# Masks by TensorE, late scaling and signs by ScalarE in the first steps of a fused attention and two-layer kernel

## The chip, the cores and the metric

The kernel runs on one core of one Trainium2 chip. The metric is the device time of one execution in microseconds; below it is the median of three runs. The profile is of one execution of its own.

## The reference

Three layers follow each other. Attention with 4 batches, 8 heads, 576 tokens and 64 dimensions keeps for each query the 32 largest scores; a dense layer of 512 to 2048 to 512 with a gated activation follows, and then a layer of eight experts, of which each token takes one.

```python
scores = scale * np.matmul(q, k.transpose(0, 1, 3, 2))
kth = np.partition(scores, -top_k, axis=-1)[..., -top_k:-top_k + 1]
scores = np.where(scores >= kth, scores, -1000000000.0)
scores = scores - np.max(scores, axis=-1, keepdims=True)
attn = np.exp(scores)
attn = attn / (np.sum(attn, axis=-1, keepdims=True) + 1e-09)
x = np.matmul(attn, v)                      # then tokens x 512
h = x @ w_in
g = h * np.clip(h + 3.0, 0.0, 6.0) / 6.0
x = g @ w_out
# experts: argmax of normalised logits; out = gate * (relu(x @ w1[e]) @ w2[e])
```

The dense layer's weights are float64 and are turned into float32 on the chip, as a rounded high part and a low part.

## The kernel before

The attention is cut into 72 units of 128 queries and two heads. A loop of 76 steps runs as a pipeline over them: step i scores unit i, selects the 32 largest of unit i−1, prepares the mask of unit i−2, takes the exponentials of units i−2 and i−3, turns the result of unit i−4 by transposes. In odd steps the products with v of units i−5 and i−4 are made. Eight units fill 256 tokens of x, which then go through the dense layer in eight pieces, one a step; so TensorE gets its main work from step 12 on. The expert layer follows after the loop.

The order of instructions is written out by hand: each step runs through a list of names, `FIRST` in steps 0 to 11, `MID` to step 20, then `ODD` and `THEN`. Each engine takes its instructions strictly in that order, and SyncE issues the DMAs in that order.

The names that matter here, with their lines: `score0`, `score1` (L435, TensorE) make the scores of half the keys for both heads in the one PSUM tile `ps_sc`; `take0`, `take1` (L446, ScalarE) copy them to the unit's tile `s`; `pairs` (L455 to L459, five VectorE operations) compares the halves and so needs `take1` and the second half in PSUM; `pick0` to `pick3` (L474, L477, VectorE) select; `bounds` (L482, L484, GpSimd) turns the 32nd largest into a bias. `bend` (L488, ScalarE) writes z, which is 0 for a kept score and huge for another one; `mask` (L492, GpSimd) subtracts z from s; `expo` (L498, ScalarE) takes the exponential in place and sums each row; `guard` (L502) and `inverse` (L505) invert the sums; `scale` (L512, ScalarE for the first 16 units) multiplies the row. `turn` (L525, TensorE) and `keep` (L530, ScalarE) transpose by way of two PSUM banks; `values` (L543, TensorE) multiplies by v; `xh` (L560, ScalarE) and `xl` (L575, VectorE) split the product.

In the same steps the float64 weights come in pieces of 128x512, one a step in steps 0 to 2 and then two, as pairs of 32-bit words. `load` fetches a piece; `one` (L241, VectorE) shifts the high word by three bits and clears the top two bits; `two` (L248, VectorE) merges sign and top exponent bit; `round` (L256, ScalarE) scales the low word to a rounding count; `add` (L261, GpSimd) adds it. One step later `hi` (L269, ScalarE) rounds to the high part, `low` (L273, GpSimd) subtracts, and `store` (L277) writes the low part to DRAM. The four buffers `wf` that `one` writes come free when the store of two steps' earlier piece has landed.

Of the kernel before, what the change touches and what calls it, by code (L numbers as in the profile page):

```python
# [38 lines left out]
EARLY = 16  # L39
PLAIN = 1  # L40
# [3 lines left out]
FIRST = ("hi0 s10 expo0 lows hi1 turn0 one0 s11 s20 low0 round0 two0 ship keep0 turn1 expo1 guard bend0 keep1 add0 turn2 load0 "  # L44
         "store0 one1 load_k inverse keep2 prep mask0 pick0 round1 score0 gate take0 scale two1 bend1 load_q swish large values xh "
         "score1 pick1 pick2 aside s21 add1 load1 xl pick3 need_v low1 take1 store1 pairs mask1 bounds small")
MID = ("lows turn0 hi0 turn1 low0 s10 s11 ship keep0 one0 keep1 expo0 two0 pick0 load_k turn2 store0 one1 pick1 expo1 hi1 guard "
       "round0 bend0 two1 score0 pick2 keep2 low1 s20 take0 gate bend1 inverse add0 score1 values take1 round1 scale swish mask0 "
       "large s21 add1 xh pick3 need_v prep xl mask1 load_q bounds small store1 load0 load1 pairs aside")
# [49 lines left out]
def layers(tc: tile.TileContext, qt, kt, v, w_in, w_out, embt, tau, w1, w2, out, y_dram, yq_dram, g_dram, tbl, xq_dram, lo_dram, flag, pools, consts):  # L99
# [33 lines left out]
    ps_y = st.enter_context(tc.tile_pool(name="ps_y", bufs=2, space=PSUM))  # L133
    ps_t = st.enter_context(tc.tile_pool(name="ps_t", bufs=1, space=PSUM))
    bank_h = ps_h.tile([128, 512], F32, name="bank_h")
    bank_a = Held(ps_a, consts).tile([128, 2, CH], F32, name="bank_a")
# [85 lines left out]
    def w_load(n):  # L222
        src, dst = wpairs[n]
        single = src.dtype == F32
        if single:
            raw = stg.tile([128, 2, 256], F32, tag="st", name="w32")
            nc.sync.dma_start(out=raw, in_=src)
        else:
            raw = stg.tile([128, 512, 2], I32, tag="st", name="w64")
            nc.sync.dma_start(out=raw.rearrange("p (a n) two -> p a n two", a=2), in_=src.bitcast(I32).rearrange("p a (n two) -> p a n two", two=2))  # L230
        ent_[n] = dict(dst=dst, raw=raw, single=single, rounded=True)

    def w_one(n):
        e = ent_[n]
        raw = e["raw"]
        e["both"] = mp.tile([128, DM], F32, tag="wf", name="wf", bufs=4)
        if e["single"]:
            nc.vector.tensor_copy(e["both"], raw.rearrange("p a n -> p (a n)"))
            return
        e["words"] = t = e["both"].bitcast(I32)  # L240
        nc.vector.tensor_scalar(t, raw[:, :, 1], 3, 0x3FFFFFFF, op0=ALU.logical_shift_left, op1=ALU.bitwise_and)  # L241

    def w_two(n):
        e = ent_[n]
        if e["single"]:
            return
        raw, t = e["raw"], e["words"]
        nc.vector.scalar_tensor_tensor(t, raw[:, :, 1], -0x40000000, t, op0=ALU.bitwise_and, op1=ALU.bitwise_or)  # L248
        if not e["rounded"]:
            nc.vector.scalar_tensor_tensor(t, raw[:, :, 0], 29, t, op0=ALU.logical_shift_right, op1=ALU.bitwise_or)  # L250

    def w_round(n):
        e = ent_[n]
        if e["rounded"] and not e["single"]:
            raw = e["raw"]
# [276 lines left out]
    avs = {}  # L532

    def values(i):
# [3 lines left out]
        avs[i] = av = half_a()[:, :128]  # L538
# [23 lines left out]
    def finish_low(i):  # L562
# [10 lines left out]
        c = slice(128 * (t % 2), 128 * (t % 2) + 128)  # L573
        xh, xl = [x[:, p, c] for x in xt[b, t // 2]]
        nc.vector.tensor_tensor(xl, av, xh.bitcast(F32), op=ALU.subtract)  # L575
        if p == 3 and t % 2:
# [11 lines left out]
    def push_group(X, gs):  # L588
# [292 lines left out]
    def step(i, last):  # L881
# [15 lines left out]
        def after(o):  # L897
            if last:
# [6 lines left out]
                   pairs=lambda: at_(0, pairs), values=lambda: both(values), xh=lambda: both(finish), xl=lambda: both(finish_low))  # L905
# [30 lines left out]
    if True:  # L936
        last = None
        with tc.manual_schedule():
# [6 lines left out]
            make_identity(nc, ident)  # L945
            nc.vector.memset(half, 0.5)
# [453 lines left out]
```

## Time and profile before

| | |
|---|---|
| median of three runs | 1007.87 us (1005.36 to 1010.01) |
| profiled execution | 1007.83 us |
| its span | 1005.8 us |
| TensorE busy in the span | 934.8 us, 93% |
| VectorE | 778.1 us, 77% |
| ScalarE | 712.8 us, 71% |
| GpSimd | 637.9 us, 63% |

The shares are means over stages with different limits. In the first tenth of the span VectorE, ScalarE and GpSimd are busy almost throughout and TensorE about half the time; from 175 us on TensorE is. The span is from the first to the last instruction; the execution's own time is 2.03 us longer.

### The profile page before, as it was taken

To read this page: it belongs to the slowest core of one execution; us is meant where nothing else is said; L and a number is where in the kernel's file an instruction comes from. 1 tells how busy PE (TensorE), PEld (TensorE's weight loads), DVE (VectorE), ACT (ScalarE), POOL (GpSimd) and SP (SyncE) were. 2 spreads that over 40 slices of the span, in tenths; PEclk is the share of its full clock that TensorE was granted. 3 is DMA by queue.
4 is the path that set the end of the run, shared out by engine and by line. 5 is a ranking of instruction groups with operands and counts; after the bars stand their busy time and mean duration, and the time that the engine had idled before them with its cause. 6 is when DMAs were issued, how large, how long until landed. Compare 5 with 4: busy or idle time off the path is not lost. (4 is left out here: it accounts for less than half of the span.)

```text
span 1005.8 us, 20687 instructions
## 1 busy us (share of the span) xinstructions
PE 934.8 (93%) x7128; PEld 820.3 (82%) x7128; DVE 778.1 (77%) x2364; ACT 712.8 (71%) x1441; POOL 637.9 (63%) x786
## 2 busy tenths in 40 slices
PE   3656688999999999999999999999999999999997
PEld 1433467989899899998998988889898988999986
DVE  7999999899989989989989899882134354666660
ACT  5899889888889788789778787785335454555551
POOL 5889899677778788688788666665333453134210
PEclk9966799999999999999999999999999999999998
DMA  7655676664456754456665476477586467767730
GB/s 251 211 177 162 213 237 234 207 202 149 141 168 195 249 184 131 137 189 192 221 177 146 143 227 202 139 237 203 172 262 223 133 226 263 242 200 239 255 124 23
DMA packets 100689, 193.21 MB, mean 192 GB/s; under 512 B 16189, under 2 KB 42448, under 8 KB 100575
## 3 DMA queue, kind: packets, MB, share of 16 engines
q1 hardware_dynamic: 95983, 181.74, 56.3%
q0 software_dynamic: 4448, 10.00, 3.2%
q8 instruction: 58, 0.95, 0.4%
q14 instruction: 56, 0.46, 0.1%
q10 hardware_dynamic: 144, 0.07, 0.0%
HBM read 163.64 MB, written 24.92 MB: 187 GB/s over the span
## 5 line engine op out<-in xcount | busy, mean ns | idle before, releaser
L492 POOL TENSOR_TENSOR s<-s,z 128x576 f32<-128x576 f32 x144 | 191.4, 1330 | 61.6 <-ACT z L488 61.0
L607 PE MATMUL bank_h<-xh,vh 128*128 128x256 f32 x576 | 171.6, 298 | 0.0
L607 PE MATMUL bank_h<-xh,lo 128*128 128x256 f32 x576 | 163.7, 284 | 0.0
L607 PE MATMUL bank_h<-xl,vh 128*128 128x256 f32 x576 | 163.6, 284 | 0.0
L474 DVE MAX8 A<-left 128x8 f32<-128x288 f32 (+1 forms) x288 | 159.5, 594 | 0.0
L525 PE MATMUL bank_t<-both,s 128*128 128x128 f32 x648 | 108.1, 290 | 30.8 <-ACT pt L530 18.1
L525 PEld LDWEIGHTS bank_t<-both,s 128*128 128x128 f32 x648 | 81.2, 148 | 53.2 <-ACT pt L530 24.2
L530 ACT COPY pt<-bank_t 128x384 f32<-128x384 f32 x216 | 101.5, 478 | 26.2 <-PE bank_t L525 26.2
L626 POOL TENSOR_TENSOR gl<-u,gh 128x512 fp32r<-128x512 f32 x72 | 93.1, 1293 | 41.6 <-ACT gh L623 41.5
L642 PE MATMUL y<-wh,gh 128*128 128x512 f32 x288 | 116.5, 405 | 0.0
L488 ACT ACTIVATE z<-s,nb 128x576 bf16<-128x576 f32 x144 | 112.2, 780 | 4.4 <-POOL nb L482 4.3
L446 ACT COPY s<-ps_sc 128x576 f32<-128x576 f32 x143 | 92.3, 645 | 32.5 <-PE ps_sc L439 11.0
L498 ACT ACTIVATE s<-s,nb 128x576 f32<-128x576 f32 x144 | 113.0, 786 | 1.5 <-POOL s L492 1.5
L642 PE MATMUL y<-lo,gh 128*128 128x512 f32 x288 | 113.5, 394 | 0.0
L642 PE MATMUL y<-wh,gl 128*128 128x512 f32 x288 | 113.2, 393 | 0.0
L607 PEld LDWEIGHTS bank_h<-xl,vh 128*128 128x128 f32 x576 | 111.2, 193 | 0.3
L607 PEld LDWEIGHTS bank_h<-xh,vh 128*128 128x128 f32 x576 | 111.1, 193 | 0.3
L607 PEld LDWEIGHTS bank_h<-xh,lo 128*128 128x128 f32 x576 | 110.7, 192 | 0.0
L1038 POOL DMA_INDIRECT out_dram<-ob,idt x21 | 25.8, 1228 | 123.4 <-ACT ob L1031 92.3
L514 POOL TENSOR_SCALAR s<-s,sums 128x576 f32<-128x576 f32 x112 | 82.5, 748 | 20.7 <-DVE sums L505 20.2
L543 PE MATMUL bank_a<-pt,vt 128*64 128x128 f32 (+1 forms) x1600 | 93.7, 275 | 0.9 <-ACT pt L530 0.9
L615 ACT ACTIVATE u<-bank_h,half 128x512 f32<-128x512 f32 x72 | 50.0, 694 | 61.8 <-PE bank_h L607 61.8
(266 smaller groups left out, 2611.6 us busy)
## 6 DMA issues: line engine op xcount, KB each, us to landing
lo<-lo_dram SPq DMA_DIRECT2D x144, 512.0 KB, 4.6
a<-in_moe_w_dram SPq DMA_DIRECT2D x64, 512.0 KB, 6.1
vt<-in_v_dram SPq DMA_DIRECT2D x28, 320.0 KB, 4.4
w<-in_moe_w_in_dram SPq DMA_DIRECT2D x16, 512.0 KB, 3.9
w<-in_moe_w_out_dram SPq DMA_DIRECT2D x16, 512.0 KB, 4.3
lo_dram<-wf SPq DMA_DIRECT2D x32, 256.0 KB, 2.7
qraw<-in_q_dram SPq DMA_DIRECT2D x48, 128.0 KB, 2.9
krs<-in_k_dram SPq DMA_DIRECT2D x16, 288.0 KB, 4.7
```

Of the source, the lines that this page charges most:

```text
L446: nc.scalar.copy(sbuf[i % NS][:, :, HS * g:HS * g + HS], ps_[i][:, :, :HS])
L474: nc.vector.max(A[:, n, 8 * r:8 * r + 8], src[:, n, :w])
L488: nc.scalar.activation(zb_[n], tile_of(i, n), AF.Relu, bias=sel[i][1][:, n, 1:2], scale=-BIG)
L492: nc.gpsimd.tensor_tensor(s, s, zb_[n], op=ALU.subtract)
L498: nc.scalar.activation(s, s, AF.Exp, bias=sel[i][1][:, n, 0:1], scale=SCALE, accum_out=sums[i][:, n:n + 1])
L514: nc.gpsimd.tensor_scalar(x, x, rv[:, n:n + 1], 1.0, op0=ALU.mult, op1=ALU.mult)
L525: nc.tensor.transpose(pp[:, 128 * k:128 * k + 128], e[:, 128 * (3 * c + k):128 * (3 * c + k) + 128], ident)
L530: nc.scalar.copy(pts[i][:, 3 * c:3 * c + 3, :].rearrange("p k n -> p (k n)"), tb_.pop((i, c))[:, :384])
L543: nc.tensor.matmul(av[64 * n:64 * n + 64, c0:c1], vt[:, k, 64 * n:64 * n + 64], pt[:, k + 5 * n if k < 4 else 4, c0:c1], start=(o == 0), s ...
L607: nc.tensor.matmul(ph[:, a, :], w, x[:, k, :], start=(k == 0 and n == 0), stop=(k == 3 and n == 2))
L626: nc.gpsimd.tensor_tensor(state[q][1], state.pop((q, "u")).rearrange("p (a n) -> p a n", a=2), state[q][0].bitcast(F32), op=ALU.subtract)
L642: nc.tensor.matmul(state["y"][o], x[:, a, c], w, start=(f == 0 and n == 0), stop=(f == 15 and n == 2))
```

## The change

It has four parts, all in steps 0 to 11.

For the first nine units (`VEILED`) the mask is put on by TensorE, under the new name `veil`: s times the identity plus z times the negative identity (in `tri`, whose later contents come at step 24) into the PSUM tile `bank_y`, 288 columns at a time; the exponential reads that tile. `bank_y` is one tile of two banks and takes the place of the two buffers of the dense layer's output. Both heads' masks use it in turn.

For the first eight units (`NORMED`) the exponentials are not scaled. `values` also multiplies the inverted sums, broadcast, by the identity, so that the other half of its PSUM bank holds the factor for each query; `xh` copies product and factor together, `xl` multiplies them on GpSimd, and the new `xe` splits the result, on ScalarE and GpSimd.

For eight weight pieces (`SIGNED`, the second piece in steps 3 to 10) `two` runs on ScalarE: a sign pass gives plus or minus 1.0, `round` adds 2^23, and the bits of both, added to the shifted word by two GpSimd operations, make up sign and top bits.

`FIRST` has another order: `low0` stands behind `add0`, `inverse` behind `pick0`, `veil1` behind `turn0`, and `veil0` between `score0` and the copy.

```diff
+NORMED = 8
+SIGNED = tuple(range(4, 20, 2))
+VEILED = 9
...
-FIRST = ("hi0 s10 expo0 lows hi1 turn0 one0 s11 s20 low0 round0 two0 ship keep0 turn1 expo1 guard bend0 keep1 add0 turn2 load0 "
+FIRST = ("hi0 s10 expo0 lows hi1 turn0 veil1 one0 s11 s20 round0 two0 ship keep0 turn1 expo1 guard bend0 keep1 add0 low0 turn2 load0 "
...
-    ps_y = st.enter_context(tc.tile_pool(name="ps_y", bufs=2, space=PSUM))
+    ps_y = st.enter_context(tc.tile_pool(name="ps_y", bufs=1, space=PSUM))
+    bank_y = ps_y.tile([128, 2, DM], F32, name="bank_y")
...
+        if e["signed"]:
+            nc.vector.tensor_scalar(t, raw[:, :, 1], 3, None, op0=ALU.logical_shift_left)
+            return
...
+        if e["signed"]:
+            nc.scalar.activation(raw[:, :, 1].bitcast(F32), raw[:, :, 1], AF.Sign)
+            return
         nc.vector.scalar_tensor_tensor(t, raw[:, :, 1], -0x40000000, t, op0=ALU.bitwise_and, op1=ALU.bitwise_or)
...
-            nc.scalar.activation(raw[:, :, 0], raw[:, :, 0].bitcast(U32), AF.Copy, scale=2.0 ** -29)
+            nc.scalar.activation(raw[:, :, 0], raw[:, :, 0].bitcast(U32), AF.Copy, bias=2.0 ** 23 if e["signed"] else 0.0, scale=2.0 ** -29)
...
-            nc.gpsimd.tensor_tensor(e["words"], e["words"], e["raw"][:, :, 0], op=ALU.add)
+            for k in (1, 0) if e["signed"] else (0,):
+                nc.gpsimd.tensor_tensor(e["words"], e["words"], e["raw"][:, :, k], op=ALU.add)
...
+    def veil(i, n):
+        if i >= VEILED:
+            return
+        s = tile_of(i, n)
+        for g in range(2):
+            c = slice(HS * g, HS * g + HS)
+            nc.tensor.matmul(bank_y[:, g, :HS], ident, s[:, c], start=True, stop=False)
+            nc.tensor.matmul(bank_y[:, g, :HS], tri, zb_[n][:, c], start=False, stop=True)
...
     def expo(i, n):
...
-        s = tile_of(i, n)
-        nc.scalar.activation(s, s, AF.Exp, bias=sel[i][1][:, n, 0:1], scale=SCALE, accum_out=sums[i][:, n:n + 1])
+        s = x = tile_of(i, n)
+        if i < VEILED:
+            s, x = s.rearrange("p (g c) -> p g c", g=2), bank_y[:, :, :HS]
+        nc.scalar.activation(s, x, AF.Exp, bias=sel[i][1][:, n, 0:1], scale=SCALE, accum_out=sums[i][:, n:n + 1])
...
     def scale(i):
+        if i < NORMED:
+            return
...
+        if i < NORMED:
+            sh = both_[:, 128:]
+            halves[i] = both_
+            rv = sums.pop(i)
+            for n in range(2):
+                nc.tensor.matmul(sh[64 * n:64 * n + 64, :], rv[:, n:n + 1].broadcast_to([128, 64]), ident, start=True, stop=True)
...
     def finish(i):
...
+        if i < NORMED:
+            nc.scalar.copy(norm_[:, i % 2, :], halves.pop(i))
+            return
...
     def finish_low(i):
...
+        if i < NORMED:
+            x = norm_[:, i % 2, :]
+            nc.gpsimd.tensor_tensor(x[:, :128], x[:, :128], x[:, 128:], op=ALU.mult)
+            return
...
+    def finish_early(i):
+        if i >= NORMED:
+            return
+        x = norm_[:, i % 2, :128]
...
+        nc.scalar.copy(xh, x)
+        nc.gpsimd.tensor_tensor(xl, x, xh.bitcast(F32), op=ALU.subtract)
...
-                state["y"] = [ps_y.tile([128, DM], F32, tag="y", name="y") for _ in gs]
+                state["y"] = [bank_y[:, o, :] for o in range(len(gs))]
...
+            nc.gpsimd.tensor_scalar(tri, ident, -1.0, None, op0=ALU.mult)
```

Where this puts the work, engine by engine. TensorE in an odd step, before: third transpose (L525), first score (L435), two units' values (L543), second score.

```order
L525 MATMUL bank_t_122<-both,s_146 128x128 x3
L435 MATMUL ps_sc<-kpl,qpl 128x288 x2
L543 MATMUL bank_a<-pt,vt 64x128 x20
L435 MATMUL ps_sc<-kpl,qpl 128x288 x2
L525 MATMUL bank_t_123<-both,s_147 128x128 x3
```

And after, at the same place (L551 transposes, L446 scores, L507 and L508 the mask, L572 the factors, L577 values):

```order
L551 MATMUL bank_t_123<-both,s_149 128x128 x3
L446 MATMUL ps_sc<-kpl,qpl 128x288 x2
L507 MATMUL bank_y<-s_147,both 128x288
L508 LDWEIGHTS tri
L508 MATMUL bank_y<-z_152,tri 128x288
...
L572 MATMUL bank_a<-both,sums 64x128 x2
L577 MATMUL bank_a<-pt,vt 64x128 x10
L572 MATMUL bank_a<-both,sums 64x128 x2
L577 MATMUL bank_a<-pt,vt 64x128 x10
L446 MATMUL ps_sc<-kpl,qpl 128x288 x2
L551 MATMUL bank_t_124<-both,s_146 128x128 x3
```

Between the two scores there stand now a mask of the next unit (shown for one of its two halves) and the factors; the other head's mask stands behind the first transpose.

ScalarE from the second rounding to the end of an odd step, before: rounding (L256), first copy (L446), both scalings (L512), z (L488), two casts (L560), second copy.

```order
L256 ACTIVATE w_437<-w_437 128x512
L446 COPY s_146<-ps_sc 128x2x288
L512 ACTIVATE s_147<-s_147,sums 128x576 x2
L488 ACTIVATE z_152<-s_148,nb 128x576
L560 CAST xh<-bank_a 128x128 x2
L446 COPY s_146<-ps_sc 128x2x288
```

And after (L266 rounding, L457 copies, L256 the sign, L499 z, L584 product and factor, L629 the split):

```order
L266 ACTIVATE w_453<-w_453 128x512
L457 COPY s_147<-ps_sc 128x2x288
L256 ACTIVATE w_453<-w_453 128x512
L499 ACTIVATE z_153<-s_149,nb 128x576
L584 COPY norm<-bank_a 128x256 x2
L457 COPY s_147<-ps_sc 128x2x288
L629 CAST xh<-norm 128x128 x2
```

The scalings are gone, the sign pass is in their place, and the split has moved behind the second copy.

GpSimd in a step, before: a sum's guard (L502), add (L261), mask (L492), add, low part (L273), mask, bounds (L482, L484), low part.

```order
L502 TENSOR_SCALAR sums<-sums 128x2
L261 TENSOR_TENSOR wf<-wf,w_400 128x512
L492 TENSOR_TENSOR s_148<-s_148,z_151 128x576
L261 TENSOR_TENSOR wf<-wf,w_437 128x512
L273 TENSOR_TENSOR wf<-wf,wh 128x512
L492 TENSOR_TENSOR s_148<-s_148,z_152 128x576
L482 TENSOR_TENSOR nb<-A,kb 128x4
L484 TENSOR_TENSOR viol<-A 128x4
L273 TENSOR_TENSOR wf<-wf,wh 128x512
```

And after, in an even step (L526 guard, L272 adds, L284 low parts, L493 and L495 bounds):

```order
L526 TENSOR_SCALAR sums<-sums 128x2
L272 TENSOR_TENSOR wf<-wf,w_502 128x512
L284 TENSOR_TENSOR wf<-wf,wh 128x512
L272 TENSOR_TENSOR wf<-wf,w_567 128x512 x2
L284 TENSOR_TENSOR wf<-wf,vh 128x512
L493 TENSOR_TENSOR nb<-A,kb 128x4
L495 TENSOR_TENSOR viol<-A 128x4
```

The masks are gone, the second piece has two adds, and the first low part now stands behind the first add; in odd steps two products (L613) stand ahead of the second low part and two subtractions (L630) behind it.

## Rows read from the trace of the kernel before

**Rows 1.** busy us by engine (PE, PEld, DVE, ACT, POOL), then PEclk, DMA, GB/s

```profile
50.00:62.50 12.50, 5.40 (x25) 3.03 (x23) 12.40 (x38) 12.50 (x27) 11.91 (x14) 0.70 0.52 164
...
175.00:200.00 25.00, 24.96 (x199) 22.72 (x198) 22.46 (x82) 21.21 (x49) 17.48 (x25) 1.00 0.62 214
```

**Rows 2.** VectorE in order of time: start, us, line, operation, out<-in, shapes

```profile
22.97 0.45 DVE L455 TENSOR_TENSOR ps_sc<-ps_sc,s 128x288 f32<-128x288 f32 x1
...
49.52 0.48 DVE L575 TENSOR_TENSOR xl<-bank_a,xh 128x128 fp32r<-128x128 f32 x2
...
51.25 0.45 DVE L455 TENSOR_TENSOR ps_sc<-ps_sc,s 128x288 f32<-128x288 f32 x1
...
53.50 0.42 DVE L241 TENSOR_SCALAR wf<-w 128x512 int32<-128x512 int32 x1
...
55.95 0.73 DVE L248 SCALAR_TENSOR_TENSOR wf<-w,wf 128x512 int32<-128x512 int32 x1
...
56.61 0.51 DVE L474 MAX8 A<-top 128x8 f32<-128x144 f32 x2
...
60.49 0.44 DVE L455 TENSOR_TENSOR ps_sc<-ps_sc,s 128x288 f32<-128x288 f32 x1
...
109.19 0.45 DVE L455 TENSOR_TENSOR ps_sc<-ps_sc,s 128x288 f32<-128x288 f32 x1
...
111.95 1.64 DVE L248 SCALAR_TENSOR_TENSOR wf<-w,wf 128x512 int32<-128x512 int32 x1
```

**Rows 3.** ScalarE in order of time, steps 5 and 6

```profile
49.05 0.43 ACT L560 CAST xh<-bank_a 128x128 fp32r<-128x128 f32 x2 [1.14 <-PE bank_a L543]
...
49.73 0.64 ACT L446 COPY s<-ps_sc 128x576 f32<-128x576 f32 x1 [0.25 <-PE ps_sc L435]
...
50.27 0.62 ACT L269 CAST wh<-wf 128x512 fp32r<-128x512 f32 x1
...
55.16 0.68 ACT L256 ACTIVATE w<-w 128x512 int32<-128x512 uint32 x1
...
56.25 1.45 ACT L512 ACTIVATE s<-s,sums 128x576 f32<-128x576 f32 x2
...
57.60 0.78 ACT L488 ACTIVATE z<-s,nb 128x576 bf16<-128x576 f32 x1
...
58.78 0.64 ACT L269 CAST vh<-wf 128x512 fp32r<-128x512 f32 x1
```

**Rows 4.** TensorE in order of time: scores (L435), values (L543), transposes (L525)

```profile
43.84 1.33 PE L435 MATMUL ps_sc<-kpl,qpl 64*128 64x288 f32 x4 [0.95 <-PE bank_t L525]
...
48.93 0.76 PE L435 MATMUL ps_sc<-kpl,qpl 64*128 64x288 f32 x4
...
64.18 4.53 PE L543 MATMUL bank_a<-pt,vt 128*64 128x128 f32 x40
...
119.49 1.54 PE L525 MATMUL bank_t<-both,s 128*128 128x128 f32 x6 [4.91 <-ACT s L512]
...
127.58 2.41 PE L543 MATMUL bank_a<-pt,vt 128*64 128x128 f32 x40
```

**Rows 5.** GpSimd in order of time, step 6: a mask and an add

```profile
56.10 1.72 POOL L492 TENSOR_TENSOR s<-s,z 128x576 f32<-128x576 f32 x1
...
57.79 1.29 POOL L261 TENSOR_TENSOR wf<-wf,w 128x512 int32<-128x512 int32 x1
```

**Rows 6.** DMA issues from 30 to 110 us: count, KB each, median us to landing

```profile
lo_dram<-wf SPq DMA_DIRECT2D x16, 256.0 KB, 2.4
```

**Rows 7.** TensorE by half microseconds: us, busy (count), clock, DMA, GB/s

```profile
68.00:68.50 0.50, 0.50 (x8) 0.50 0.53 213
...
68.50:69.00 0.50, 0.50 (x6) 0.82 0.04 16
...
70.50:71.00 0.50, 0.00 (x0) 1.00 0.79 287
...
72.00:72.50 0.50, 0.00 (x0) 0.59 0.73 279
```

More of the change, by code (lines that the diff above doesn't have):

```diff
@@ L43 @@
 RAMP, MOES, WORDS = 3, 12, 21
-FIRST = ("hi0 s10 expo0 lows hi1 turn0 one0 s11 s20 low0 round0 two0 ship keep0 turn1 expo1 guard bend0 keep1 add0 turn2 load0 "
-         "store0 one1 load_k inverse keep2 prep mask0 pick0 round1 score0 gate take0 scale two1 bend1 load_q swish large values xh "
-         "score1 pick1 pick2 aside s21 add1 load1 xl pick3 need_v low1 take1 store1 pairs mask1 bounds small")
+FIRST = ("hi0 s10 expo0 lows hi1 turn0 veil1 one0 s11 s20 round0 two0 ship keep0 turn1 expo1 guard bend0 keep1 add0 low0 turn2 load0 "
+         "store0 one1 load_k keep2 prep pick0 inverse round1 score0 veil0 mask0 gate take0 scale two1 bend1 load_q swish large values xh "
+         "score1 pick1 pick2 aside s21 add1 load1 xl pick3 need_v low1 take1 store1 pairs xe mask1 bounds small")
 MID = ("lows turn0 hi0 turn1 low0 s10 s11 ship keep0 one0 keep1 expo0 two0 pick0 load_k turn2 store0 one1 pick1 expo1 hi1 guard "
        "round0 bend0 two1 score0 pick2 keep2 low1 s20 take0 gate bend1 inverse add0 score1 values take1 round1 scale swish mask0 "
-       "large s21 add1 xh pick3 need_v prep xl mask1 load_q bounds small store1 load0 load1 pairs aside")
+       "large s21 add1 xh pick3 need_v prep xl mask1 load_q bounds small store1 load0 load1 pairs xe aside")
 THEN = ("lows pick0 turn0 expo0 keep0 ship expo1 pick1 bend0 s10 guard turn1 place pick2 inverse score0 mask0 turn2 s11 take0 "
@@ L230, in w_load @@
             nc.sync.dma_start(out=raw.rearrange("p (a n) two -> p a n two", a=2), in_=src.bitcast(I32).rearrange("p a (n two) -> p a n two", two=2))
-        ent_[n] = dict(dst=dst, raw=raw, single=single, rounded=True)
+        ent_[n] = dict(dst=dst, raw=raw, single=single, rounded=True, signed=not single and n in SIGNED)
     def w_one(n):
@@ L496, in expo @@
             sums[i] = sm.tile([128, 2], F32, tag="sums", name="sums")
-        s = tile_of(i, n)
-        nc.scalar.activation(s, s, AF.Exp, bias=sel[i][1][:, n, 0:1], scale=SCALE, accum_out=sums[i][:, n:n + 1])
+        s = x = tile_of(i, n)
+        if i < VEILED:
+            s, x = s.rearrange("p (g c) -> p g c", g=2), bank_y[:, :, :HS]
+        nc.scalar.activation(s, x, AF.Exp, bias=sel[i][1][:, n, 0:1], scale=SCALE, accum_out=sums[i][:, n:n + 1])
     def guard(i):
@@ L530, in keep @@
         nc.scalar.copy(pts[i][:, 3 * c:3 * c + 3, :].rearrange("p k n -> p (k n)"), tb_.pop((i, c))[:, :384])
-    avs = {}
+    avs, halves = {}, {}
+    norm_ = mp.tile([128, DM], F32, tag="ug", name="norm", bufs=1).rearrange("p (i n) -> p i n", i=2)
     def values(i):
@@ L537, in values @@
         pt = pts.pop(i)
-        avs[i] = av = half_a()[:, :128]
+        both_ = half_a()
+        avs[i] = av = both_[:, :128]
+        if i < NORMED:
[4 more added lines that the diff above has]
+                nc.tensor.matmul(sh[64 * n:64 * n + 64, :], rv[:, n:n + 1].broadcast_to([128, 64]), ident, start=True, stop=True)
         vs = [(V[u[1], u[3]], 0, 128)] if u[0] == "t" else [(V[u[1], u[2] + a], 64 * a, 64 * a + 64) for a in range(2)]
@@ L573, in finish_low @@
         c = slice(128 * (t % 2), 128 * (t % 2) + 128)
+        if i < NORMED:
+            x = norm_[:, i % 2, :]
+            nc.gpsimd.tensor_tensor(x[:, :128], x[:, :128], x[:, 128:], op=ALU.mult)
+            return
         xh, xl = [x[:, p, c] for x in xt[b, t // 2]]
         nc.vector.tensor_tensor(xl, av, xh.bitcast(F32), op=ALU.subtract)
+        if p == 3 and t % 2:
+            push_group(xt[b, t // 2], [4 * b + t - 1, 4 * b + t])
+    def finish_early(i):
+        if i >= NORMED:
+            return
+        x = norm_[:, i % 2, :128]
+        _, b, t, p = units[i]
+        if p == 0 and t % 2 == 0:
+            xt[b, t // 2] = [xp.tile([128, 4, 256], F32R, tag=n, name=n) for n in ("xh", "xl")]
+        c = slice(128 * (t % 2), 128 * (t % 2) + 128)
+        xh, xl = [x[:, p, c] for x in xt[b, t // 2]]
+        nc.scalar.copy(xh, x)
+        nc.gpsimd.tensor_tensor(xl, x, xh.bitcast(F32), op=ALU.subtract)
         if p == 3 and t % 2:
@@ L904, in step @@
                    guard=lambda: at_(3, guard), inverse=lambda: at_(3, inverse), scale=lambda: at_(3, scale), bounds=lambda: at_(1, bounds),
-                   pairs=lambda: at_(0, pairs), values=lambda: both(values), xh=lambda: both(finish), xl=lambda: both(finish_low))
+                   pairs=lambda: at_(0, pairs), values=lambda: both(values), xh=lambda: both(finish), xl=lambda: both(finish_low), xe=lambda: both(finish_early))
+        for n in range(2):
+            ops["veil" + str(n)] = lambda n=n: at_(2 + n, veil, n)
         for name, j, f, n in (("bend", 2, relu, 2), ("mask", 2, mask, 2), ("expo", 3, expo, 2), ("pick", 1, select, 4),
```

## The prediction

> **What bounds the kernel now.** I read the stages first, then one step of each engine. From 50 to 62.5 us VectorE is busy 12.40 of 12.50 us, ScalarE all of it and GpSimd 11.91, TensorE 5.40; from 175 us TensorE takes over, 24.96 of 25 us [rows 1]. So time won early moves the TensorE-bound rest forward, as long as nothing between gives it back. A step is read from VectorE's pair comparisons, which come once per unit: unit 2's start at 22.97 and unit 11's at 109.19, nine steps in 86.22 us [rows 2]. These nine steps are all that the change touches; the order view shows every engine's instructions as they were from step 12 on.
>
> In them VectorE does not wait: in step 6 its comparisons run from 51.25 to 60.49, 9.24 us of work one behind the other [rows 2]. ScalarE's step 6 runs from 50.27 to 58.78, 8.51 us, also without a hole [rows 3]. In odd steps a third chain comes close: comparisons over, score matmul, two units' values, second score, ScalarE's copy, next comparisons. In step 5 it takes 43.84 to 49.73 plus 0.64, so 50.37, and the comparisons start at 51.25: 0.9 us to spare [rows 2, 3, 4].
>
> **The change, part by part.** VectorE loses eight sign merges. From the start of one to the start of what follows is 56.61 − 55.95 = 0.66 us, so 8 × 0.66 = 5.3 us; and four pairs of xl, 0.48 us each, 1.9 us [rows 2]. It gains nothing. With nothing else late, the nine steps would take 86.2 − 7.2 = 79.0 us, 8.58 us a step from step 3 to 10.
>
> ScalarE loses the two scalings, 57.60 − 56.25 = 1.35 us a step, and gains a sign pass of the shape of its rounding pass, 0.68 us [rows 3]: 8.51 − 1.35 + 0.68 = 7.84 us in even steps. In odd steps two 128x256 copies replace two casts of 128x128 (0.43 us for both [rows 3]) and two casts from SBUF are added: between nothing and twice 0.43 more for each kind, I take 0.43 for each, so 8.7. That is level with VectorE's 8.58. The exponential now reads PSUM; its price may move either way and I leave it as it is. No table load is added for the sign function: the order has the same number of them.
>
> GpSimd loses two masks a step, the first of 57.79 − 56.10 = 1.69 us, and gains one add of 1.29 us, in odd steps also four 128x128 operations, each between nothing and 1.29 [rows 5]; at a third, 1.7 us. It has less to do than before in every step and stays hidden. What moves is when: its last low part now stands behind both adds, the first of which waits for the sign pass near the end of ScalarE's step. Two more adds and the low part (3.8 us) behind a sign pass that ends some 1.2 us before the step does put the store 2.6 us into the next step, and a store lands 2.4 us after its issue [rows 6]. VectorE's second piece needs that buffer some 3.4 us into the step (2.25 us of comparisons, 53.50 − 51.25 [rows 2], and one piece): a new wait of up to 1.6 us in odd steps, little in even ones. Queued behind it are all selections of that step. In odd steps TensorE's chain, below, is as late, so I count it once.
>
> TensorE gets the masks: per unit and head two fp32 matmuls of 288 columns and two bf16. The nearest row is a score, two fp32 matmuls of 288 columns on half the array each: 0.76 us at one level of the clock, 1.33 at the other [rows 4]. So a mask costs from 0.76 (bf16 free, full overlap) to 2.3 us (no overlap, bf16 at half), or 1.33 to 4.0 cold; I take 1.4 and 2.45, nearer the low end since a score holds all the same columns. The row sums are four matmuls of the values' kind, whose twenty a step (forty records) take 2.41 warm and 4.53 cold [rows 4]: 0.5 or 0.9 us.
>
> Where these lie decides. The odd steps' chain was score, values, score, copy; now it is score, mask, sums, values, score, copy. Warm: 0.76 + 1.4 + 0.5 + 2.41 + 0.76 + 0.64 = 6.5 us, with 2.25 us of comparisons and two hand-overs of 0.25 us (as long as ScalarE waited for the second score at 49.73 [rows 3]) 9.2 us; and the score is itself queued behind a mask that waits for an exponential on ScalarE, which I put at one hand-over more: 9.5 us instead of VectorE's 8.58. Cold: 1.33 + 2.45 + 0.9 + 4.53 + 1.33 + 0.64 = 11.2, with comparisons and two hand-overs 13.9 us. Even steps have no values: 8.58 us and 0.2 for the store, 8.8.
>
> Which level holds? The granted clock is 0.50 (1.2 GHz) at 68.00 us; it rose in the half microsecond after 68.50, TensorE being busy without a break with the values that began at 64.18, and fell in the one after 72.00, TensorE having idled from 70.50 on [rows 4, 7]. The changed kernel keeps TensorE busy through most of an odd step, but it still idles about 2 us in each step until the first exponential is done. So I expect the high level in most of an odd step and a fall in some of the gaps; for that I add half of what separates a warm mask from a cold one, (2.45 − 1.4)/2 = 0.5 us, to a pair of steps.
>
> The sum: steps 3 to 5, 51.25 − 22.97 = 28.28 before, become 8.6 + 9.2 (step 4, with the first transposes and a cold mask, I leave as it is) + 9.5 = 27.3, gain 1.0. The three pairs from 6 to 11 took (109.19 − 51.25)/3 = 19.3 each and become 9.5 + 8.8 + 0.5 = 18.8, gain 1.5. Together 2.5 us of the 7.2 that VectorE sheds. I take off 0.8 us, 0.1 in each of eight steps, because GpSimd now works at the moment when VectorE handles its pieces: 1.7 us gained. Step 12's first hidden matmuls now wait for xl from GpSimd; TensorE has 4.91 us of idle time in that step [rows 4], so this costs nothing; without that cover it would cost about the two subtractions, under 1 us. The profiled execution took 1007.83 us, span 1005.8; 1007.83 − 1.7 = 1006.1, and the median of the runs, 1007.87, is the same number.
>
> A row bears on that 0.8 us. A sign merge took 1.64 us at 111.95, not 0.73, while GpSimd worked [rows 2]. The Trainium skill, "SBUF — State Buffer" (SBUF: two separate sides), says that VectorE and GpSimd share a pair of ports as an exclusive lock, held for a whole instruction by whoever starts first, against VectorE's two-input operations among others; the trace agrees in that row, by its length. By that rule each step's one remaining merge could be held up whenever a low part runs, which gives the third rival below.
>
> **Rivals.** *VectorE's pace holds* (0.21): the masks cost TensorE under 1 us and the clock stays high, so the odd chain stays under 8.6 us. Then the nine steps take 79 to 81 us and the time is 1001 to 1003; I put 1001.5. For it: three engines are relieved at once, and TensorE is busy 43% there [rows 1]. Against it: only 0.9 us was to spare and two items are put into that chain.
>
> *Slower: TensorE stays at 1.2 GHz* (0.19). The masks' fp32 passes at half speed make the odd step 13.9 us and the even one, whose second exponential waits for a cold mask, 8.8 + 2.45 − 1.4 = 9.9: 23.8 a pair, 4.5 over, 13.5 us in three pairs, 1021.3. Half of the time low gives 6.8 us, 1014.6, which I put here. It decides from a pair of over 19.3 us, so from 0.5 us more than I forecast. For it: the clock was low in most of this stretch before.
>
> *Held-up VectorE* (0.07): the merge waits for GpSimd, or the second piece for its store, on the path. At 1.64 − 0.73 = 0.9 us in each of eight steps, 7.3 us; against the 1.7 gained that is 5.6 slower, 1013.4.
>
> *The forecast* (0.53): the work leaves VectorE, but the odd steps' TensorE chain takes its place as the bound, and 1 to 4 us of 7.2 arrive.
>
> **How the numbers follow.** Predicted: 1006.1. About 0.5%, 5 us, is what a measurement of this kernel can tell from no change, so the forecast is "the same". Faster by more is the first rival, 0.21; slower by more are the second and third, 0.26; the same, 0.53. The range runs from the first rival's time, with its floor of 7.2 us, to the second's half-way case: 1000.8 to 1015. Left out are a wholly cold ramp and, below, a gain that VectorE's work does not hold.
>
> **What would show it.** In the changed profile: unit 11's comparisons at about 107.5 us, 84.5 us behind unit 2's; VectorE with holes in odd steps, ended by ScalarE's copy of the second score, or at its second piece by a store; GpSimd at under 10.5 of 12.5 us; TensorE at over 8 of 12.5 between 50 and 100 us; steps 12 on as long as before. Comparisons 8.6 us apart in odd steps too would show the first rival right; a score of 1.33 us in most odd steps, pairs of over 20 us and 1.2 GHz through most of 50 to 110 us the second; a merge of over 1 us in each step the third. If the ramp gains and the end does not, something between 110 and 175 us gave it back, and I have that wrong.

## The result, and the profile after

The changed kernel takes 1020.74 us (median of six runs, 1019.21 to 1022.89) against 1007.06 for the kernel before: 1.0136 times as long, with an interval of 1.0121 to 1.0150. It is 13.7 us slower, where 1.7 us faster was forecast and 1015 was the upper end. The profiled execution took 1020.79 us, its span is 1018.7. One of the ten executions of the run after_both, below, took 1866.76 us and is left out of its ratio.

The two stretches of [rows 1], in the changed kernel, with the same columns:

```profile
50.00:62.50 12.50, 8.41 (x42) 4.83 (x36) 12.07 (x42) 9.72 (x23) 9.09 (x13) 0.86 0.48 159
...
175.00:200.00 25.00, 24.60 (x207) 21.41 (x205) 22.08 (x79) 23.05 (x49) 20.87 (x28) 1.00 0.73 237
```

ScalarE and GpSimd have become free by 2.8 us each in the first stretch, TensorE has taken on 3.0, and its granted clock is 0.86 there instead of 0.70. VectorE, which had 12.40, has holes.

The loss comes in two parts. The comparisons tell the first. Unit 2's start at 23.52 (before: 22.97), unit 11's at 113.96:

```profile
23.52 0.47 DVE L466 TENSOR_TENSOR ps_sc<-ps_sc,s 128x288 f32<-128x288 f32 x1 [0.20 <-ACT s L457]
...
113.96 0.44 DVE L466 TENSOR_TENSOR ps_sc<-ps_sc,s 128x288 f32<-128x288 f32 x1
```

That is nine steps in 90.44 us instead of 86.22. At unit 18 the lag is 189.42 − 183.98 = 5.4 us; 0.55 of it stands at unit 2 already, and that start differs by more between the traces below (22.9 to 24.1). The second part comes where the order of instructions is the same as before: the copies of the dense layer's output, once per group of 256 tokens, start 5.5 us later than before in the first group (218.30 against 212.84) and 11.2 us later in the last one in the loop (729.29 against 718.11). At the end of the span it is 12.9.

**The first part: VectorE waits for a store.** VectorE's waits from 14 to 115 us (line, tile, who was waited for: us in total, times, longest):

```profile
DVE wf L246 <- DMA lo_dram<-wf: 5.4, 5, 2.2
DVE wf L248 <- DMA lo_dram<-wf: 1.6, 1, 1.6
DVE sums L529 <- POOL sums L526: 1.0, 2, 0.6
DVE wf L246 <- DMA w<-in_moe_w_out_dram: 0.4, 1, 0.4
DVE ps_sc L466 <- ACT s L457: 0.4, 2, 0.2
```

The first two rows, 7.0 us, are the shift of a weight piece that waits until the low part of the piece that had its buffer is in DRAM. Before, no such wait is recorded. Only the last row is what was forecast: comparisons that wait for ScalarE's copy of the second score. One odd step, all engines in order of time (start us, us, engine, line, operation, tiles, shapes, count, idle time before and who ended it):

```profile
41.88 0.45 DVE L466 TENSOR_TENSOR ps_sc<-ps_sc,s 128x288 f32<-128x288 f32 x1
...
43.11 1.28 POOL L284 TENSOR_TENSOR wf<-wf,vh 128x512 fp32r<-128x512 f32 x1
...
44.42 0.33 SPq L288 DMA_DIRECT2D lo_dram<-wf  x1
...
45.29 0.76 PE L446 MATMUL ps_sc<-kpl,qpl 64*128 64x288 f32 x4
...
45.98 0.75 PE L507 MATMUL bank_y<-s,both 128*128 128x288 f32 x2
...
47.12 1.28 POOL L284 TENSOR_TENSOR wf<-wf,vh 128x512 fp32r<-128x512 f32 x1
...
47.39 0.44 PE L572 MATMUL bank_a<-both,sums 128*64 128x128 f32 x4
...
47.63 1.05 DVE L246 TENSOR_SCALAR wf<-w 128x512 int32<-128x512 int32 x1 [2.20 <-DMA lo_dram<-wf]
...
50.16 0.76 PE L446 MATMUL ps_sc<-kpl,qpl 64*128 64x288 f32 x4
...
50.96 0.64 ACT L457 COPY s<-ps_sc 128x576 f32<-128x576 f32 x1
...
53.52 0.44 DVE L466 TENSOR_TENSOR ps_sc<-ps_sc,s 128x288 f32<-128x288 f32 x1
```

The comparisons of unit 4 start at 41.88. GpSimd's last low part of the step before starts only 1.23 us later, and its store is issued 2.54 us into the step. VectorE comes to the shift at 45.43 and waits 2.20 us. Then the shift takes 1.05 us instead of 0.42, and it ends 0.28 us after GpSimd's next low part (47.12 + 1.28 = 48.40). TensorE's chain runs beside this: first score, mask, factors, values, second score, and ScalarE's copy is done at 51.60. The next comparisons start at 53.52 without a wait: VectorE was later than the chain by 1.9 us.

VectorE's account for the nine steps: 7.0 us for stores, 1.8 in the other rows above, and 3.2 for weight operations that took longer than a shift of 0.42 or a merge of 0.69 (1.6 in the second pieces of steps 3 to 10, eight at 0.61 on average; 1.1 for the second piece of step 11, whose shift took 1.53; 0.5 in the first pieces). What is left of the 90.4 is 78.4 us of work; the prediction's sum for it was 79.0.

**The second part: TensorE waits for a copy.** End of a group of the dense layer in the changed kernel, second output bank, TensorE and ScalarE:

```profile
217.88 0.39 PE L697 MATMUL bank_y<-wh,gl 128*128 128x512 f32 x1
...
218.30 0.58 ACT L715 COPY ysb<-bank_y 128x512 f32<-128x512 f32 x1 [0.22 <-PE bank_y L697]
...
218.94 0.50 PE L697 MATMUL bank_y<-wh,gh 128*128 128x512 f32 x1 [0.68 <-ACT ysb L715]
...
220.63 0.59 ACT L715 COPY ysb<-bank_y 128x512 f32<-128x512 f32 x1 [1.75 <-PE bank_y L697]
```

And TensorE's two longest rows of waits from 200 us on:

```profile
PE bank_y L697 <- ACT ysb L715: 6.0, 8, 1.3
PE bank_y L697 <- ACT ysl L709: 0.7, 1, 0.7
```

Both output banks are now one tile. The products of the second half, which write the second bank, wait until ScalarE has read the first one. From one half's copy to the other's it takes 2.33 us. The same place in the kernel before (L642 makes the products, L660 copies, `y` is one of two buffers):

```profile
212.84 0.59 ACT L660 COPY ysb<-y 128x512 f32<-128x512 f32 x1 [0.21 <-PE y L642]
...
212.86 0.39 PE L642 MATMUL y<-lo,gh 128*128 128x512 f32 x1
...
213.09 0.39 PE L642 MATMUL y<-wh,gl 128*128 128x512 f32 x1
...
214.20 0.59 ACT L660 COPY ysb<-y 128x512 f32<-128x512 f32 x1 [0.77 <-PE y L642]
```

There it was 1.36 us. The difference, 0.97 us, comes in nearly every group: six of the seven gaps from group to group are longer by 0.9 to 1.0 us. The program has this wait in its list of waits, where the kernel before has none at that place:

```
L697 MATMUL bank_y<-wh,gh 128x512 [waits Activation_49]
```

The chip doesn't ask for it: the Trainium skill, "PSUM — Partial Sum Buffer" (Summary: rules for kernel authors), says that PSUM may be read while a matmul runs if the matmul writes another bank. In the kernel before the trace agrees: the first half's copy, 212.84 to 213.43, runs beside products into the other bank.

### The profile page after: what moved, and what is told of

Same layout as the page of the kernel before. It is cut to its first block, busy times and chain, and to the rows that moved or that the text cites. A ratio compares the mean times of both kernels' runs of the same rounds, so it can differ in the third digit from the quotient of the medians.

```text
span 1018.7 us, 20919 instructions
## 1 busy us (share of the span) xinstructions
PE 956.9 (94%) x7268; PEld 831.0 (82%) x7268; DVE 774.5 (76%) x2348; ACT 709.4 (70%) x1441; POOL 629.9 (62%) x793
## 5 line engine op out<-in xcount | busy, mean ns | idle before, releaser
L514 POOL TENSOR_TENSOR s<-s,z 128x576 f32<-128x576 f32 x126 | 164.6, 1308 | 61.4 <-ACT z L499 60.6
L697 PE MATMUL bank_y<-wh,gh 128*128 128x512 f32 x288 | 117.5, 408 | 6.7 <-ACT ysb L715 6.0
L457 ACT COPY s<-ps_sc 128x576 f32<-128x576 f32 x143 | 92.1, 644 | 33.7 <-PE ps_sc L450 11.3
L499 ACT ACTIVATE z<-s,nb 128x576 bf16<-128x576 f32 x144 | 112.2, 779 | 4.4 <-POOL nb L493 4.3
L551 PE MATMUL bank_t<-both,s 128*128 128x128 f32 x648 | 105.1, 283 | 10.2 <-ACT s L538 9.5
L697 PE MATMUL bank_y<-lo,gh 128*128 128x512 f32 x288 | 113.6, 394 | 0.0
L697 PE MATMUL bank_y<-wh,gl 128*128 128x512 f32 x288 | 113.3, 393 | 0.0
L551 PEld LDWEIGHTS bank_t<-both,s 128*128 128x128 f32 x648 | 80.2, 145 | 30.9 <-ACT s L538 12.7
L522 ACT ACTIVATE s<-s,nb 128x576 f32<-128x576 f32 x126 | 98.9, 786 | 1.0 <-POOL s L514 1.0
L577 PE MATMUL bank_a<-pt,vt 128*64 128x128 f32 (+1 forms) x1600 | 87.9, 265 | 0.6 <-ACT pt L556 0.6
```

The lines of the kernel that those rows point to most:

```text
L457: nc.scalar.copy(sbuf[i % NS][:, :, HS * g:HS * g + HS], ps_[i][:, :, :HS])
L499: nc.scalar.activation(zb_[n], tile_of(i, n), AF.Relu, bias=sel[i][1][:, n, 1:2], scale=-BIG)
L522: nc.scalar.activation(s, x, AF.Exp, bias=sel[i][1][:, n, 0:1], scale=SCALE, accum_out=sums[i][:, n:n + 1])
L551: nc.tensor.transpose(pp[:, 128 * k:128 * k + 128], e[:, 128 * (3 * c + k):128 * (3 * c + k) + 128], ident)
L577: nc.tensor.matmul(av[64 * n:64 * n + 64, c0:c1], vt[:, k, 64 * n:64 * n + 64], pt[:, k + 5 * n if k < 4 else 4, c0:c1], start=(o == 0), s ...
L697: nc.tensor.matmul(state["y"][o], x[:, a, c], w, start=(f == 0 and n == 0), stop=(f == 15 and n == 2))
```

## The experiments

The interval stands behind each ratio to the kernel before, which ran on the same chip each time. The runs came from more than one chip, and the kernel before took 1007 to 1014 us on them, so only ratios are compared. "Ramp" below is the time from unit 2's comparisons to unit 11's: 86.2 before, 90.4 after.

### One tile for both output banks

```diff
-    ps_y = st.enter_context(tc.tile_pool(name="ps_y", bufs=2, space=PSUM))
+    ps_y = st.enter_context(tc.tile_pool(name="ps_y", bufs=1, space=PSUM))
+    bank_y = ps_y.tile([128, 2, DM], F32, name="bank_y")
...
-                state["y"] = [ps_y.tile([128, DM], F32, tag="y", name="y") for _ in gs]
+                state["y"] = [bank_y[:, o, :] for o in range(len(gs))]
```

> The kernel before, with one change: the dense layer's two output banks are one tile, as in the changed kernel. Theory A (one tile makes the first product of a group's second half wait for ScalarE's copy of the first half, about 0.9 us in each of eight groups): 1007.1 + 7.5 = 1014.6 us. Theory B (the late loss of the changed kernel follows from its slower first steps, and the tile alone costs nothing): 1007 us, within 1.5.

1.0095 (1.0061 to 1.0130), so 9.6 us slower; ramp 86.6. TensorE's first row of waits from 200 us on is the one of the changed kernel:

```profile
PE bank_y L643 <- ACT ysb L661: 6.0, 8, 1.3
```

This part of the change alone, put into the kernel before, costs 6.2 to 13.1 us by the interval; its middle is over half of the whole loss of 13.7. Theory A holds; the interval takes in its 7.5 us.

The reverse, the changed kernel with both copies behind the second half's products:

```diff
-                if q == 7:
-                    out_y(o)
+                if q == 7 and o == len(gs) - 1:
+                    for p in range(len(gs)):
+                        out_y(p)
```

> The changed kernel, with both copies of a group's dense output behind the second half's products, so that no product of that group waits for a copy. Theory A: 1020.7 - 7.5 = 1013.2 us, and the ramp as it was (unit 11's comparisons 90.4 us behind unit 2's). Theory B: 1020.7, within 1.5.

1.0062 (1.0037 to 1.0088), 1013.3 us on the scale of the result (the ratio times 1007.06 us), so the time is theory A's. The trace says that only a part of it comes from the copies. The wait at the products is gone, but groups stand 73.2 us apart (217.47 and 290.69), against 73.7 with the wait and 72.7 before. Two copies in a row on ScalarE now delay a copy that the next transposes need:

```profile
PE bank_t L551 <- ACT pt L556: 1.9, 6, 0.3
```

So this mends only half of it. The rest seems to lie in the ramp: its instructions are those of the changed kernel, but it took 89.1 us in this trace instead of 90.4, with 5.3 us of waits for stores instead of 7.0. A ramp read from one trace thus differs by 1 us or more with no edit in it, and smaller differences of ramps below say nothing.

Giving the masks' tile up after step 11 and allocating two single banks then mends the second part whole:

```diff
+    vs, late_y = ExitStack(), {}
+    bank_y = vs.enter_context(tc.tile_pool(name="ps_v", bufs=1, side="right", space=PSUM)).tile([128, 2, DM], F32, name="bank_y")
...
+        if i == VEILED + 2:
+            vs.close()
+            late_y["p"] = mb.enter_context(tc.tile_pool(name="ps_y", bufs=2, side="right", space=PSUM))
```

> The changed kernel, but the PSUM tile of the masks is given up after step 11 and the dense layer has its two single output banks again, as in the kernel before. Theory A (a group's second half waits for the copy because both halves are one tile): no wait of TensorE at the dense layer's second products, groups 72.7 us apart as before instead of 73.5, and only the first steps' loss is left: 5.5 us slower than the kernel before, 0.5%. Theory B (the late loss has another cause): 11 us or more slower, over 1%.

1.0038 (1.0016 to 1.0060), by the ratios some 10 us less than the changed kernel (1.0136). Groups are 72.7 us apart again (217.84 and 290.57), and no wait for `ysb` is left. What remains is the ramp, 88.4 us here, with 5.3 us of waits for stores:

```profile
DVE wf L246 <- DMA lo_dram<-wf: 3.6, 5, 1.2
DVE wf L248 <- DMA lo_dram<-wf: 1.7, 1, 1.7
```

### The wait for the store

More buffers: the eight signed pieces go into `gh` and `gl`, which are idle until step 12.

```diff
+        if n in SPARE:
+            e["both"] = mp.tile([128, DM], F32, tag="gh" if n % 4 else "gl", name="wg", bufs=2)
+        else:
+            e["both"] = mp.tile([128, DM], F32, tag="wf", name="wf", bufs=4)
```

> The changed kernel, with the eight signed weight pieces in the four buffers gh and gl, which the dense layer needs only from step 12 on: a piece's buffer then comes free four steps later instead of two, and VectorE waits for no store in steps 3 to 10. Theory A (VectorE's wait for the store, 7.0 us in all, is what the first steps lose): odd steps about 8.7 to 9.0 us, unit 2 to unit 11 about 81 us, time 1020.7 - 9.5 = 1011. Theory B (the odd steps' chain on TensorE of the forecast is as late as the store): odd steps stay at 9.5 to 10 us or more, unit 2 to unit 11 about 85 us, time 1015.

> The changed kernel with late copies and with the four further buffers. Theory A: 1020.7 - 7.5 - 9.5 = 1003.7 us, faster than the kernel before by 3. Theory B of the first steps: 1007.5 us.

1.0074 (1.0051 to 1.0097) with the four buffers alone, 1.0042 (1.0011 to 1.0073) with late copies as well. On the scale of the result these are 1014.5 us, near theory B's 1015, and 1011.3, slower than both theories said. The ramp falls to 84.7 and 84.4 us. No wait for a store is left in steps 3 to 11, and now the forecast's wait shows. VectorE's waits from 14 to 115 us in after_both:

```profile
DVE ps_sc L470 <- ACT s L461: 1.6, 3, 0.9
DVE sums L533 <- POOL sums L530: 1.3, 2, 0.7
DVE wg L250 <- DMA w<-in_moe_w_in_dram: 0.4, 1, 0.4
```

So the store's wait did cost the ramp some 6 us, and behind it the odd steps' chain is the next one late; but it is late by 1.2 us a step at most (with the four buffers alone). In the traces the gain doesn't reach the dense layer whole: with the four buffers unit 11 is 6.3 us earlier than in the changed kernel, the first group's copy 2.7 (215.60 and 218.30). Step 12 took 11.9 us and step 13 12.2, in the changed kernel 11.4 and 11.1. GpSimd is busy 11.7 and 12.05 us in these two steps, in the changed kernel 11.2 and 9.9, so it fills them. It does the same in no_signs, below, which has no further buffers; why GpSimd has more to do there was not pursued. (By the ratios, taken on different chips, the four buffers gain 6.2 us in all.)

Without further buffers: both low parts at the start of a step, on top of after_two_tiles.

```diff
-... keep0 turn1 expo1 guard bend0 keep1 add0 low0 turn2 load0 store0 one1 ... xl pick3 need_v low1 take1 store1 pairs ...
+... keep0 turn1 low0 low1 expo1 guard bend0 keep1 add0 turn2 load0 store0 store1 one1 ... xl pick3 need_v take1 pairs ...
```

> As after_two_tiles, and in steps 0 to 11 GpSimd computes both low parts at the start of a step, ahead of the guard of the sums, and their stores follow each other. VectorE's wait for the store (7.0 us in nine steps) goes, without any further buffer. Theory A (the store wait lay on top of the odd steps' chain on TensorE, which then bounds): odd steps 9.8 to 10.2 us, even ones 8.6 to 9.2, unit 2 to unit 11 84 to 85 us, time 1 to 2 us below the kernel before. Theory B (the store wait alone was the loss): odd steps 8.7 us, unit 2 to unit 11 80 us, time 5 to 6 us below the kernel before.

0.9995 (0.9971 to 1.0019): level with the kernel before. No wait for a store is left, but the ramp is 87.3 us, worse than either theory said, and from step 4 on odd steps are no longer than even ones (9.6 to 10.0 both). VectorE's groups of merges (L256) and first shifts (L246) from 23 to 98 us, with busy us and mean ns:

```profile
L256 DVE SCALAR_TENSOR_TENSOR wf<-w,wf 128x512 int32<-128x512 int32 x8 | 9.4, 1170 | 0.3
...
L246 DVE TENSOR_SCALAR wf<-w 128x512 int32<-128x512 int32 x8 | 6.9, 866 | 0.0
```

A merge that takes 0.69 us by itself takes 1.17, a shift 0.87 instead of 0.42. With the second shifts, 3.4 us, that makes 19.7 us where eight of each need 12.2: 7.5 us in nine steps. Neither theory had named this; it is the prediction's third rival, GpSimd holding VectorE up.

### TensorE's odd chain, and VectorE held by GpSimd

On top of low_parts_early the values go behind the second score, and their copies and the split into the next step.

```diff
-... large values xh score1 pick1 pick2 aside s21 add1 load1 xl pick3 ...
+... large score1 values pick1 pick2 aside s21 add1 load1 pick3 ...
```

> As low_parts_early, and in steps 0 to 10 the values stand behind the second score on TensorE, their copies and the split in the next step. Theory A (in odd steps the comparisons wait for a second score that stands behind factors and values): odd steps 8.7 to 9.1 us like even ones, unit 2 to unit 11 80 to 81 us, time 5 us below the kernel before. Theory C (what makes odd steps of after_both 10 us is VectorE held up by GpSimd, or ScalarE being full): odd steps stay at 9.8 us or more, unit 2 to unit 11 84 us or more.

0.9972 (0.9957 to 0.9988), 2.8 us faster than the kernel before. The ramp is 84.9 us, with 0.2 us of waits in all, so VectorE works without a hole, and steps 4 to 11 take 9.2 to 10.1 us, odd and even alike. Theory A's 80 us is missed by 5. Theory C's 84 us and its cause, VectorE held up by GpSimd, are what the trace shows, though most odd steps stay under the 9.8 us that it named. VectorE's first shifts from 23 to 98 us, 1.05 us each instead of 0.42:

```profile
L247 DVE TENSOR_SCALAR wf<-w 128x512 int32<-128x512 int32 x8 | 8.4, 1047 | 0.0
```

GpSimd's low part and VectorE's shift in one step, from the two engines' lists:

```profile
70.97 1.28 POOL L283 TENSOR_TENSOR wf<-wf,vh 128x512 fp32r<-128x512 f32 x1
```

```profile
71.51 1.02 DVE L247 TENSOR_SCALAR wf<-w 128x512 int32<-128x512 int32 x1
```

The low part ends at 72.25 and the shift 0.28 us later, at 72.53, as if most of its 0.42 us had been done only then. The Trainium skill, "SBUF — State Buffer" (Who interferes with whom), says that VectorE's copies, casts and tensor_scalar operations can take the port pair that GpSimd also needs, and that whoever comes second is blocked until the other's instruction is over. The trace agrees by these durations; the comparisons of 288 columns, with one operand in PSUM, stay at 0.42 to 0.47 us here and in the other traces.

Moving the first piece's shift and merge ahead of the comparisons, and one low part behind the first add:

```diff
+            at = names.index("pairs")
+            names[at:at] = ["next1", "next2"]
+            ops.update(next1=lambda: pair(w_one, -1, 0), next2=lambda: pair(w_two, -1, 0))
```

> As values_late, and VectorE shifts and merges a step's first weight piece ahead of the comparisons of the step before instead of behind them, with one of GpSimd's two low parts put off behind the first add. Theory E (in values_late VectorE's shift took 1.02 to 1.47 us instead of 0.42 because it was held until GpSimd's low part was over, and this is what keeps the steps at 9.2 to 10 us): shifts of about 0.42 us, steps of 8.6 to 8.8 us, unit 2 to unit 11 80 us instead of 84.9, time 7 us below the kernel before. Theory F (the shifts' length is cover; ScalarE or TensorE would be as late): unit 2 to unit 11 84 us or more, 3 us below the kernel before, and VectorE waits for ScalarE's copies instead.

1.0009 (0.9993 to 1.0025), ramp 86.6: worse than values_late. Now the merge meets an add of GpSimd and the bounds:

```profile
40.79 1.34 POOL L271 TENSOR_TENSOR wf<-wf,w 128x512 int32<-128x512 int32 x1
...
41.02 1.66 DVE L257 SCALAR_TENSOR_TENSOR wf<-w,wf 128x512 int32<-128x512 int32 x1
...
42.09 0.65 POOL L492 TENSOR_TENSOR nb<-A,kb 128x4 f32<-128x4 f32 x1
```

The bounds, otherwise 0.20 us, take 0.65 while the merge runs: the hold works both ways. This run didn't separate E from F, since the hold moved and did not go. So GpSimd's work itself was taken away:

```diff
         hi, x = parts_of(ent_[n])
+        if 3 <= n < 19:
+            return
         nc.gpsimd.tensor_tensor(x.bitcast(F32R), x, hi.bitcast(F32), op=ALU.subtract)
```

> As values_late, but the low parts of sixteen weight pieces (those of steps 3 to 10) are left out: GpSimd does not subtract, and what is stored as low part is the whole weight, so that the dense layer computes with other weights; only steps 3 to 11 are read, not the time. Theory E (VectorE's shifts are held by the low part that GpSimd works on at that moment): the shift behind the comparisons takes 0.42 to 0.6 us instead of 1.05 on average, steps of 8.6 to 8.8, unit 2 to unit 11 79 to 81 us instead of 84.9. Theory F (the length of the shifts is cover for another bound): unit 2 to unit 11 84 us or more, and VectorE waits for ScalarE or TensorE.

Every step from 3 to 9 takes 8.55 to 8.58 us, odd ones as well as even ones, and the ramp 79.9 us, a last step of 11.0 us with two merges in it included. Comparisons and the weight operations of one step in VectorE's list, and the group of the first shifts:

```profile
65.83 0.45 DVE L467 TENSOR_TENSOR ps_sc<-ps_sc,s 128x288 f32<-128x288 f32 x1
...
68.08 0.42 DVE L247 TENSOR_SCALAR wf<-w 128x512 int32<-128x512 int32 x1
68.53 0.69 DVE L257 SCALAR_TENSOR_TENSOR wf<-w,wf 128x512 int32<-128x512 int32 x1
69.14 0.42 DVE L245 TENSOR_SCALAR wf<-w 128x512 int32<-128x512 int32 x1
...
74.39 0.45 DVE L467 TENSOR_TENSOR ps_sc<-ps_sc,s 128x288 f32<-128x288 f32 x1
...
L247 DVE TENSOR_SCALAR wf<-w 128x512 int32<-128x512 int32 x10 | 4.2, 419 | 0.0
```

Theory E holds: this is the pace that the prediction worked out for VectorE, 8.58 us, and 5 us of values_late's ramp are time in which VectorE is held by GpSimd's low parts. With the values late, TensorE and ScalarE are in time for it.

### Single parts of the change

The sign merges on VectorE again, on top of after_two_tiles (`SIGNED = ()`):

> As after_two_tiles, with the sign merges on VectorE for all pieces, as in the kernel before (masks on TensorE and late scaling stay). Theory A (sign pass and second add make the low part and its store late): VectorE's waits for stores fall from 7.0 to under 2 us in nine steps, its work rises by 5.3; unit 2 to unit 11 86 to 88 us instead of 90.4, time 0 to 2 us above the kernel before. Theory D (the store is late because the low part now stands behind the masks' chain and the first add, not for the signs): waits stay at 4 us or more, unit 2 to unit 11 over 90 us, 5 us or more above the kernel before.

1.0051 (1.0028 to 1.0073), ramp 88.3. The waits for stores fall from 5.3 to 2.1 us and the merges come back, so the ramp is level: most of what the signs save VectorE is what it then waits. That lies between A and D, and neither the time nor the ramp tells it from after_two_tiles.

The masks on GpSimd again, on top of values_late (`VEILED = 0`):

> As values_late, but the masks of the first nine units are subtracted by GpSimd again, as in the kernel before. If TensorE's masks are worth their place: GpSimd gets 3.4 us more a step, 11 us in all against steps of 9.4, and bounds; unit 2 to unit 11 95 us or more, time 7 us above values_late or worse. If they are not: within 1.5 us of values_late.

1.0098 (1.0072 to 1.0124), ramp 96.5, so 12.7 us above values_late. GpSimd is busy 12.26 of 12.5 us from 75 to 87.5 us:

```profile
75.00:87.50 12.50, 4.94 (x25) 2.90 (x23) 11.12 (x32) 10.06 (x22) 12.26 (x15) 0.75 0.39 131
```

Steps take 10.9 to 11.2 us from step 7 to 10. So TensorE's masks are the part that pays: without them the other two put more on GpSimd than a step holds.

### The better version

> The same program as values_late once more, in more rounds: 2 to 4 us below the kernel before, 0.2 to 0.4%.

0.9975 (0.9964 to 0.9986), 1004.56 us against 1006.91. Two tiles, low parts at the start of the step, values behind the second score: with these the change is 2.4 us faster than the kernel before instead of 13.7 slower.

## Why the prediction was wrong

**Right: what bounds, and the prices.** VectorE sets the ramp, and 8.58 us a step is its floor (8.55 to 8.58 in no_low_parts). A mask takes 45.98 to 47.39, so 1.41 us, at the high clock, where 1.4 was taken, and 2.56 at the low one, where 2.45 was. Factors and values from 47.39 to 50.16 are 2.77 us (2.9 taken). The odd chain from the first score to the end of ScalarE's copy takes 6.31 us (6.5 taken), and from the comparisons on 51.60 − 41.88 = 9.7 (9.5). ScalarE's sign pass takes 0.70 us (0.68).

**Wrong, the first step: "so I count it once".** The wait for the store was seen, with its place, its cause and nearly its size: the store was put 2.6 us into the step and is 2.54 us into it, the need at 3.4 us and it comes at 3.55. But it was then dropped because TensorE's chain was as late. By the prediction's own numbers it wasn't: VectorE's 8.58 plus 1.6 of wait is 10.2 us, and the chain was put at 9.5. Two things that are late for the same event are compared, and the later one is taken; here it was the one left out. It also came out longer, 2.2 us, since the buffer came free 3.2 us after the issue of the store (44.42 to 47.63) where the median of [rows 6], 2.4, was used. And the even steps, 8.8 us with 0.2 for the store, came out at 9.03 to 9.08; two of them wait 0.4 us for a store.

**Wrong, the second step: 0.1 us a step for GpSimd.** The hold was priced at 0.8 us for eight steps and put in a rival with a chance of 0.07. In the changed kernel it is 3.2 us, beside the store's wait. In the two versions with more buffers it is 2.1 to 2.2 us; with the low parts at the start of a step it is 6.5 to 8.1 us and sets the ramp. The row that shows it, a merge of 1.64 us [rows 2], was read as an exception. In the kernel before the shifts took 0.47 us on average and the merges 0.72, so it was one; the change gives GpSimd another order, and this was not read from the new one.

**Wrong, the third step: "steps 12 on as long as before".** It rested on the order of instructions, which is indeed the same. But the change of `bank_y` from two buffers to one tile was told in front and never priced, and the order doesn't show waits. The question to put was who reads this tile while another half of it is written. That is 0.97 us in nearly every group, 7.4 us from the first group to the end of the span (12.9 − 5.5), more than the whole ramp lost. No rival had a loss behind step 12, and the range's upper end stood on a slow clock that didn't come.

The wait that the prediction did price there holds: step 12's first hidden matmul waits 1.2 us for xl from GpSimd, but the step takes 11.40 us where it took 11.27, so the idle time covers it. The lower end of the range, 1000.8, is 1000.6 by its own sum (1007.8 − 7.2); nothing hangs on it.

**The rivals.** TensorE at 1.2 GHz was wrong: the granted clock is 1.00 from 75 to 87.5 us (before 0.57) and 0.86 in the stretches on both sides. Before, then after:

```profile
75.00:87.50 12.50, 8.60 (x63) 6.02 (x61) 12.43 (x45) 11.97 (x24) 11.67 (x12) 0.57 0.52 158
...
75.00:87.50 12.50, 9.40 (x50) 5.72 (x51) 10.83 (x34) 12.04 (x27) 9.38 (x15) 1.00 0.56 173
```

The low stretches that remain (from 54.7 to 57.6 for instance) follow idle time of TensorE of 3.2 us, and a mask costs 1.15 us more in them (54.61 to 57.17). The third rival, VectorE held up by the store's wait or by GpSimd, was the right mechanism for the ramp, and its chance, 0.07, was the mistake. That its 5.6 us slower than before stand against 5.4 measured at unit 18 is luck: it was worked out from merges of 1.64 us, and the merges took 0.69 to 0.72 here, so its sign, a merge of over 1 us in each step, did not come. What was long were the shifts, and the waits for stores were twice as much (7.0 us against 3.2). The forecast's own mechanism exists, as after_both shows, but as the third in line.

The ramp of 84.5 us that was forecast was measured in after_both (84.4). That is not a confirmation: 1.6 us of it are waits for ScalarE's copy, and the rest above 79 is other waits (1.7) and VectorE held by GpSimd (2.1).

**What stays open.** Why GpSimd has more to do in steps 12 and 13 of some versions; what the late scaling is worth, which was not taken out by itself; and whether another place for VectorE's weight operations avoids GpSimd, since the one that was tried only met other instructions of it.

## What to carry to other kernels

Where two chains are late for the same event, write both totals down and take the larger; a wait may be left out as "covered" only if the sum with it is still below the cover. When two buffers become one tile, list who reads one half while the other is written, all through the program and not only where the edit is; the order of instructions doesn't show that. And when work moves between engines, look at what runs beside what afterwards: an instruction that was 0.42 us long next to one neighbour may be 1.0 next to another.

## What was not expected of the hardware

VectorE's one-input shift of 128x512 words, from and to SBUF, took up to 1.56 us instead of 0.42 where GpSimd was in a two-input operation of 1.28, and 0.42 in all steps from 3 to 11 of the run that left GpSimd's low parts out (no_low_parts). Merges took up to 1.66 instead of 0.69 (pieces_ahead). In values_late and its repetition nine steps lost 6.5 to 7.2 us so. In the other direction GpSimd's bounds of 0.20 us took 0.65 beside a merge (pieces_ahead).
